# One eight-bank PSUM tile in place of four two-bank tiles, sinks split by two instructions a tile, and a new order, in a fused attention and soft-MoE kernel

## The chip, the cores and the metric

The kernel runs on one core of a Trainium2 chip. The metric is the time of one execution on the device in microseconds, the median of several runs. A core has five engines with instruction queues of their own: TensorE (PE, matmuls; its weight loads are listed as PEld), VectorE (DVE), ScalarE (ACT), GpSimd (POOL) and SyncE (SP, which issues most of the DMAs here). Each queue runs in order, and the engines wait for each other by semaphores. Matmul results lie in PSUM, which has eight banks of 512 floats a partition.

## The reference

Sliding-window attention with four sinks is followed by a soft mixture of experts; all is float32. There are 4 batches, 8 heads, 768 rows of 64; window 128; 8 experts with 4 slots each, model width 512, hidden width 1024.

```python
scores = scale * np.matmul(q, k.transpose(0, 1, 3, 2))
keep = (pos[None, :] < n_sink) | ((rel >= 0) & (rel < window))
a = softmax(np.where(keep, scores, -1e9))          # rows of 768
x = (a @ v).transpose(0, 2, 1, 3).reshape(B * S, H * D)
logits = x @ phi                                    # 3072 x 32
d = softmax(logits, axis=0)                         # over the 3072 tokens
slot_input = (d.T @ x).reshape(E, S_per_e, D)
h = np.maximum(slot_input[e] @ w1[e], 0.0)          # for each expert e
slot_out[e] = h @ w2[e]
return softmax(logits, axis=1) @ slot_out           # 3072 x 512
```

## The kernel before, in words

**Attention.** The work is cut into 12 jobs, one for each batch and each block of 256 rows, with all 8 heads. A job loads its k, q and v, transposes k and q on PE in 64x64 pieces (`prep`) and lets ACT and DVE copy them out of PSUM, and then goes through four score tiles (two groups of 64 rows a head by two sets of four heads): PE makes the scores, DVE masks them and takes the maxima, ACT the exponentials, DVE the inverse sums, POOL the normalised weights (`softmax`). POOL splits the weights of the four sinks into a high and a low half (`sinks`, L917: a cast and a subtraction for each of two pairs of heads), POOL cuts the window's triangle (`select`), PE transposes the weights and the sinks (the latter into `pst`), and `values` (L956) multiplies them with v. That product goes into two banks in two phases, `part(True)` and `part(False)`, with the PE drained between them; four matmuls for the sinks (pst by `vsink`) lie between. `natural` copies the result, and `moe.tokens` (L349) makes the logits of the job's tokens, their maxima, exponentials and weighted sums.

**Tail.** Behind the last job `finish` closes the sums over the tokens, and `tail` (L553) does the experts: 128 matmuls of the hidden product, relu by ACT (L573) and DVE (L574) on two tiles, transposes on PE with copies L593, further transposes with casts L547, then 168 matmuls of the second product, a split into high and low halves (L621 on ACT, L622 on DVE), and the output. The output is 24 tiles of 128x512, each one bank and two matmuls; the copies out of PSUM (L636) are ACT's for i = 0 and DVE's for i = 1, and seven DMAs of 0.5 or 1 MB (L637) take them to memory.

**What sets the order.** A planner (`Plan`, L168 to L296) is given each step with its engines, estimated times, what it reads and writes, and a key. Its loop picks, step by step, what can start first, with the keys as priorities; the numbers in the table `CFG` shift the keys. It hands each PSUM result one of eight banks, or two neighbouring ones for a score tile. The steps are issued in that order, by L129, and so the rows of the profile have this line for nearly everything. In the tail `InOrder` takes the place of the planner: a result gets the next of banks 2 to 7 in turn. The waits between engines are found afterwards, from which instruction touches which tile.

**Banks and tiles.** The eight banks are four tiles of two (L1225), and the bank with number b is a half of tile b // 2:

```python
pools = [ps.tile([P, 2, 512], F32, name=f"ps{i}") for i in range(4)]
...
t = self.banks[b // 2]
return t if kind == "s" else t[:, b % 2]
```

In the order of the kernel before, an instruction on one bank of such a tile waits for instructions on the other bank as well, even where the two results have nothing to do with each other.

Of the kernel before, what the change touches and what calls it, by code (L numbers as in the profile page):

```python
# [73 lines left out]
def sink_values(nc, plan, pool, tmp, c, v, v4s):  # L74

    B = v.shape[0]
    v4 = tmp[0:32, 0:256].rearrange("p (b d) -> p b d", b=B)
    srow = tmp[0:32, 512:640].rearrange("p (x r q z) -> p x r q z", x=2, r=4, q=2)
    hi = tmp[:, 768:1024].bitcast(F32R)
    c.v4s = v4s  # L80

    c.bm = pool.tile([P, 4], F32, name="bm")
    low = pool.tile([P, 1], F32, name="low")
    h = plan.psum()

    def load(e):
        for b in range(B):
            nc.sync.dma_start(v4[:, b, :], v[b, :, 0:NS, :])

    def selectors(e):  # L90
        sv = c.ident[0:32, 0:32].rearrange("p (q x z) -> p x q z", q=2, x=2)
        for r in range(4):
            nc.vector.tensor_copy(srow[:, :, r], sv)
        nc.vector.reduce_sum(c.bm, c.ident.rearrange("p (w q s) -> p q w s", w=8, q=4), axis=AX.XY)
        nc.vector.reduce_sum(low, c.ident.rearrange("p (x h z) -> p h x z", x=2, h=2)[:, 1], axis=AX.XY, negate=True)
# [12 lines left out]
    plan.add(1.0, "A", 0.3, lambda e: nc.scalar.copy(hi, h["tile"][:, 0:B * 64]), r=["v4p"], w=["v4h"])  # L108
    plan.add(1.0, "V", 0.8, split, r=["v4p", "v4h", "bm"], w=["v4s"], last=h)


def batch_sinks(nc, t, c, b):
    nc.vector.tensor_tensor(
        t.rearrange("p a (h d) -> p (a h) d", h=2),
        c.v4s[b].unsqueeze(1).to_broadcast([P, 4, 64]),
        c.bm.unsqueeze(2).to_broadcast([P, 4, 64]), op=ALU.mult)
# [26 lines left out]
class Plan:  # L143
# [24 lines left out]
    def add(self, key, eng, time, fn, r=(), w=(), new=None, last=None, mode=(128, 128), size=0):  # L168

        self.sizes.append(size)  # L170
        self.steps.append((key, eng, time if isinstance(time, tuple) else (time,) * len(eng), fn,
                           tuple(r), tuple(w), self.some(new), self.some(last)))
        self.modes.append(mode)

    def order(self):
# [41 lines left out]
        while len(order) < len(steps):  # L217
            best = None
            for e, o in todo.items():
# [17 lines left out]
                if at and (best is None or t0 < best[0]):  # L237
                    if e == "P":
                        _, t, i = min((steps[i][0] + self.STAY * (self.modes[i] != mode), t, i)
                                      for t, i in at if t <= t0 + 0.1)  # L240
# [5 lines left out]
            if e == "P":  # L246
                t0 += self.SWITCH * (self.modes[i] != mode)
                mode = self.modes[i]
            _, engs, times, _, _, _, new, last = steps[i]
# [72 lines left out]
class Moe:  # L322
# [26 lines left out]
    def tokens(self, plan, keys, b, j, x, xn, blocks):  # L349
# [34 lines left out]
        plan.add(next(k), "A", 0.34,  # L384
                 lambda e: nc.scalar.activation(lt[64:128], L["tile"][64:128, 0:P], AF.Exp, bias=new[64:128],
                                                accum_out=zb[64:128]),
                 r=[L["name"], ("m", n % 2)], w=["lt1", zbn], last=L)
        if n:

            plan.add(next(k), "A", 0.19,  # L390
                     lambda e: nc.scalar.activation(al, old, AF.Exp, bias=new, scale=-1.0),
# [42 lines left out]

        plan.add(next(k), "V", 0.14, totals, r=[zbn, aln], w=["z"])
        key = next(k)
# [51 lines left out]
    def slot_softmax(self, plan, key, b, names):  # L488
# [16 lines left out]

        plan.add(key, "V", 0.7, sums, w=[n])
        plan.add(key, "V", 0.3, lambda _: nc.vector.tensor_tensor(
            e, e, rs.unsqueeze(2).to_broadcast([P, 6, 32]), op=ALU.mult), w=[n])
# [131 lines left out]
class Weights:  # L640
# [9 lines left out]
    def load(self, t):  # L650
# [5 lines left out]
        else:  # L656
# [9 lines left out]
KIND = {'kt': 'w', 'q': 'w', 'T': 'w', 'sk': 'w', 'xn': 'w', 'x': 'w'}  # L666
CFG = {'prep': [58.14, -103.97, 8.81, 76.04, -10.47, 26.64],
       'load': [-48.35, 47.19],
       'v': [57.21, 53.78],
       'S': 15.41,  # L670
       'M': -22.38,
       'E': -97.66,
       'N': -54.45,
       'K0': -25.05,
       'T': [10.2, -41.41, 69.99, -71.23, -42.73, -20.91],
       'K': [-20.3, -9.37, 32.07],
       'sel': [-5.43, -51.93, -28.52, -10.71],
       'val': [36.09, 6.74, -33.7],
       'val1': [-174.01, 24.73, -66.86],
       'xn': [44.67, -22.43, -0.05],  # L680
       'tok': [89.38, -10.2, 18.38, -35.19, -40.54, -173.09, -194.1, 86.66, 85.8, -208.04,
               6.21],
       'sm': -1.2,
       'sinks': 12.15,
       'tr': [83.07, -55.05, -13.7, 82.62, 38.72, -58.7, 23.06, 2.13, -57.09, 43.08, 8.7, 2.71,
              59.56, 30.4, -103.15, -5.02, -84.19, 23.07, 51.64, 58.39, -12.0, -151.1, 31.83,
              47.24, -18.05, -22.13, 6.38],
       'w': [156.88, 8.0],
       'fin': [8.82, 115.48, -28.65, 1.18, 38.54, -142.25, -5.87, -1.81, -63.43, 24.51],
       'xn1': [-3.39, 43.09, -33.75],  # L690
       'tok1': [-8.95, -17.67, -75.74, 15.99, -33.99, 10.77, -17.8, 44.33, 18.88, -217.71,
                -10.41]}


def window_path(ctx, tc, c, moe, q, k, v, phi, w1, w2, out):
# [29 lines left out]
    v4s = [t[:, 1584 + 64 * b:1648 + 64 * b] for b in range(3)]  # L725
    skb = t[:, 1776:2032].rearrange("p (i x r q y s) -> p i x r q y s", i=2, x=2, r=4, q=2, y=2)
    t = slot()
# [5 lines left out]
    pts.append(fr.tile([P, 4, 132], F32, name="pt"))  # L733
    vsink = fr.tile([P, 2, P], F32R, name="vsink")
    pst = fr.tile([P, 256], F32R, name="pst")
# [115 lines left out]
    def softmax(keys, n, tl):  # L851
# [85 lines left out]
    def sinks_transposed(keys, n):  # L937
        h = turned(keys[0], KIND["sk"], lambda rows, m: skb[rows, m].rearrange("p x r q y s -> p (x r q y s)"),
                   [("sk", i, x) for i in range(2) for x in range(2)], n=2)
# [16 lines left out]
    def values(keys, n):  # L956
        b, j = jobs[n]
        opened, h = pair(KIND["x"])

        def part(first, last):  # L960

            for quad in range(2):
# [5 lines left out]
                for k in range(3):  # L968
                    for r, (m, o, w) in enumerate((lower[k], upper[k])):
# [5 lines left out]
                        for y in range(2):  # L975
                            nc.tensor.matmul(bank(h, x)[64 * y:64 * y + 64, at:at + w],
                                             lhsT=vbs[rows, m % 4, 4 * quad + 2 * x + y, :],
                                             rhs=xw[rows, 2 * x + y, o:o + w], start=first and k == 0 and quad == 0,
                                             stop=last, skip_group_check=True)
# [15 lines left out]
        add(keys[0], "P", 3.5 if j else 2.9, go, r=r, w=[x["name"] for x in opened], new=opened, mode=QUARTERS, size=200)  # L995
        for x in range(2):
# [224 lines left out]
def fused(ctx, tc, q, k, v, n_sink, window, phi, w1, w2, out):  # L1221
    nc = tc.nc
    B, H = q.shape[0:2]
    ps = ctx.enter_context(tc.tile_pool(name="ps", bufs=1, space=PSUM))
    pools = [ps.tile([P, 2, 512], F32, name=f"ps{i}") for i in range(4)]  # L1225
    keep = ctx.enter_context(tc.tile_pool(name="keep", bufs=1))
# [21 lines left out]

    t = pools[3][:, 1]
    for _ in range(WARM[0]):  # L1250
# [48 lines left out]
```

## Time and profile before

| | |
|---|---|
| median of 3 runs | 273.64 us (273.29 to 274.79) |
| the profiled execution | 276.34 us |
| its span, first to last instruction | 274.2 us |
| mean granted TensorE clock | 0.896 of full |
| attention, first job's start to last job's end | about 8 to 197 us |
| end of the last job's sums (`finish`) | 197 to 207 us |
| hidden product, relu and transposes | 207 to 226 us |
| second product | 226 to 243 us |
| output stage | 243 to 271 us |

The rows further below come from one profiled execution. A row of the chain of waits says which engine's work held up the end at that time; "issue" is time in which an engine waited for nothing that the profile shows. In a row of the timeline the bracket at the end says how long the engine had been idle, and whose work ended that. "ps" is PSUM; "wt" is the common name of the rotating buffers; "first" is another.

### The profile page before, as it was taken

What the parts mean: (1) busy time and instruction counts of PE and PEld (TensorE: products, weight loads), DVE (VectorE), ACT (ScalarE), POOL (GpSimd) and SP (SyncE); (2) the same over time, 40 slices, a digit from 0 to 9 for tenths busy, and PEclk for the clock granted to TensorE, in tenths of its full rate; (3) what the DMA queues carried; (4) which work ended last, traced back from release to release, by engine and by line L of the source; (5) the groups of instructions that cost most, each with busy time, mean ns of one, the idle gap of its engine ahead of it and who ended that gap; (6) DMA issues with size and microseconds to landing.
All of it is one profiled execution on the core that took longest, in us unless ns stands there. A gap on an engine that the chain in (4) does not pass through costs nothing.

```text
span 274.2 us, 9619 instructions
## 1 busy us (share of the span) xinstructions
PE 213.4 (78%) x3756; PEld 150.6 (55%) x3756; DVE 160.2 (58%) x439; ACT 148.3 (54%) x589; POOL 155.9 (57%) x377
## 2 busy tenths in 40 slices
PE   7648999878888877897987887865889959956550
PEld 7536676666665655675766665643663323435440
DVE  3478678598898586698769798653142131033330
ACT  2474858767878776587867787843141121022320
POOL 1148879959998957699885999869140500000000
PEclk9985699999999998899999999987699999985555
DMA  5497769998977684959796987934297999015564
GB/s 135 107 197 147 202 154 336 206 348 162 256 146 217 142 250 177 217 185 217 287 191 197 186 237 207 400 93 154 65 414 247 430 410 410 24 76 200 225 267 161
DMA packets 84504, 59.51 MB, mean 217 GB/s; under 512 B 76260, under 2 KB 76260, under 8 KB 82916
## 3 DMA queue, kind: packets, MB, share of 16 engines
q1 hardware_dynamic: 84452, 58.83, 72.8%
q8 instruction: 31, 0.51, 0.8%
q14 instruction: 21, 0.17, 0.2%
HBM read 52.53 MB, written 6.29 MB: 215 GB/s over the span
## 4 chain that ended last, share of the span: by engine, by line
PE 45%; DVE 22%; ACT 12%; POOL 9%; issue 9%; DVEq 0%; ACTq 0%; POOLq 0%
PE ps L129 43%; POOL wt L129 9%; DVE wt L129 7%; ACT wt L129 6%; DVE ps L129 5%; DVE wt L636 3%; DVE first L129 3%; ACT qt L129 2%; ACT first L129 2%; PE ps L1251 1%; DVE sums L129 1%; ACT lt L129 1%; DVE acc L129 1%; DVE call L129 0%; DVE qt L129 0%
## 5 line engine op out<-in xcount | busy, mean ns | idle before, releaser
L129 PE MATMUL ps<-wt 64*64 64x192 f32 (+6 forms) x1214 | 64.0, 325 | 14.5 <-DVE wt L636 6.6
L129 POOL TENSOR_TENSOR wt<-wt 128x16 f32<-128x16 f32 (+1 forms) x108 | 53.9, 505 | 24.0 <-DVE wt L129 15.9
L129 PEld LDWEIGHTS ps<-wt 64*64 64x64 f32 (+3 forms) x1214 | 45.9, 144 | 32.3 <-issue 11.6
L129 ACT ACTIVATE wt<-ps,wt 128x132 f32<-128x132 f32 x144 | 51.3, 374 | 13.1 <-DVE wt L129 12.2
L129 POOL TENSOR_SCALAR_AFFINE_SELECT wt<-wt 128x512 f32<-128x512 f32 x88 | 53.7, 636 | 3.2 <-DVE wt L129 1.4
L129 PE MATMUL ps<-wt,qt 64*64 64x196 f32 (+2 forms) x780 | 46.1, 341 | 8.4 <-ACT qt L129 3.2
L129 PEld LDWEIGHTS ps<-wt,qt 64*64 64x64 f32 x780 | 30.0, 142 | 19.0 <-POOL wt L129 4.8
L129 PE MATMUL ps<-ident,wt 64*128 64x64 f32 (+1 forms) x370 | 29.4, 248 | 8.3 <-DVE wt L129 3.5
L129 DVE TENSOR_REDUCE wt<-ps 128x4 f32<-128x528 f32 x48 | 34.0, 707 | 1.7
L129 ACT COPY wt<-ps 128x512 f32<-128x512 f32 x38 | 22.0, 593 | 23.1 <-PE ps L129 18.3
L129 PE MATMUL ps<-ident,first 64*128 64x64 f32 (+1 forms) x560 | 26.1, 232 | 8.0 <-DVE first L129 2.1
L129 PEld LDWEIGHTS ps<-ident,wt 64*128 64x128 f32 (+1 forms) x370 | 21.7, 150 | 19.1 <-POOL wt L129 7.4
L129 ACT ACTIVATION_READ_ACCUMULATOR wt<-ps,wt 128x1 f32 x144 | 30.1, 209 | 0.0
L129 PEld LDWEIGHTS ps<-ident,first 64*128 64x128 f32 (+1 forms) x560 | 21.8, 142 | 12.5 <-issue 2.5
L129 DVE COPY wt<-ps 128x512 f32<-128x512 f32 x34 | 22.7, 686 | 9.4 <-ACT first L129 3.0
L129 DVE COPY_PREDICATED ps<-later,ps 128x256 f32<-128x256 uint8 x48 | 20.3, 422 | 2.1 <-PE ps L129 1.1
L129 ACT COPY first<-ps 128x512 f32<-128x512 f32 x26 | 14.9, 590 | 11.6 <-PE ps L129 10.4
L129 DVE COPY first<-ps 128x512 f32<-128x512 f32 x22 | 14.8, 681 | 9.9 <-PE ps L129 8.3
L636 DVE COPY wt<-ps 128x512 f32<-128x512 f32 x12 | 8.3, 692 | 15.8 <-PE ps L129 15.8
L129 ACT ACTIVATE pt<-ps,wt 128x132 f32<-128x132 f32 x48 | 17.2, 384 | 0.5 <-DVE wt L129 0.2
L636 ACT COPY wt<-ps 128x512 f32<-128x512 f32 x12 | 7.0, 585 | 17.0 <-PE ps L129 17.0
L129 PE MATMUL ps<-first,phi 128*32 128x128 f32 x384 | 14.3, 295 | 2.1 <-ACT wt L129 1.9
(118 smaller groups left out, 278.7 us busy)
## 6 DMA issues: line engine op xcount, KB each, us to landing
wt<-in_moe_w_dram SPq DMA_DIRECT2D x30, 1024.0 KB, 8.6
wt<-in_v_dram SPq DMA_DIRECT2D x24, 256.0 KB, 5.2
first<-in_k_dram SPq DMA_DIRECT2D x22, 256.0 KB, 4.8
first<-in_q_dram SPq DMA_DIRECT2D x22, 256.0 KB, 5.3
out_dram<-wt SPq DMA_DIRECT2D x5, 1024.0 KB, 4.0
first<-in_moe_w_dram SPq DMA_DIRECT2D x2, 1024.0 KB
out_dram<-wt SPq DMA_DIRECT2D x2, 512.0 KB
first<-in_k_dram SPq DMA_DIRECT2D x4, 128.0 KB, 2.4
```

The lines of the kernel that those rows point to most:

```text
L129: return self.tc.keep_in_program_order(f(*args, **kw))
L636: (nc.vector.tensor_copy if i else nc.scalar.copy)(ob[:, n - n0, i], yp)
L1251: nc.tensor.matmul(t[:, 0:P], lhsT=c.ident, rhs=c.ident, start=True, stop=True)
```

## The change

Four things change. The eight banks become one tile, and a result is a slice of it. The sinks of a score tile are split by one cast and one subtraction of twice the width, with another layout of the buffers. Their product, still four matmuls, goes in two pairs, one ahead of each phase of `values`. The planner's cost of some steps is corrected and the table of keys replaced as a whole.

```diff
-    pools = [ps.tile([P, 2, 512], F32, name=f"ps{i}") for i in range(4)]
+    pools = ps.tile([P, 8, 512], F32, name="ps")
...
     def place(self, kind, b):
-        t = self.banks[b // 2]
-        return t if kind == "s" else t[:, b % 2]
+        return self.banks[:, b:b + 2] if kind == "s" else self.banks[:, b]
...
             o = 0 if odd else 128
-            for x in range(2):
-                sk = skb[:, odd, x, :, quad]
-                src = pt[:, 2 * x:2 * x + 2, o:o + 4].unsqueeze(1).to_broadcast([P, 2, 2, 4])
-                nc.gpsimd.tensor_copy(sk[:, 0:4:2].bitcast(F32R), src)
-                nc.gpsimd.tensor_tensor(sk[:, 1:4:2], src, sk[:, 0:4:2], op=ALU.subtract)
+            sk = skb[:, odd, quad]
+            src = pt[:, :, o:o + 4].unsqueeze(1).to_broadcast([P, 2, 4, 4])
+            nc.gpsimd.tensor_copy(sk[:, 0:4:2].bitcast(F32R), src)
+            nc.gpsimd.tensor_tensor(sk[:, 1:4:2], src, sk[:, 0:4:2], op=ALU.subtract)
...
+        def sunk(first):
+
+            for r in range(2):
+                x, rows = r if first else 1 - r, slice(64 * r, 64 * r + 64)
+                nc.tensor.matmul(bank(h, x)[:, 256 * r:256 * r + 256],
+                                 lhsT=vsink[rows, 2 * x:2 * x + 2, :].rearrange("p y d -> p (y d)"),
+                                 rhs=pst[rows], start=first, stop=False, skip_group_check=True)
+
         def go(e):
-            part(True, False)
-            for quad in range(2):
-                for x in range(2):
-                    rows = slice(64 * x, 64 * x + 64)
-                    nc.tensor.matmul(bank(h, x)[:, 256 * quad:256 * quad + 256], lhsT=vsink[rows, quad, :],
-                                     rhs=pst[rows], start=False, stop=False, skip_group_check=True)
-            nc.tensor.drain()
-            part(False, True)
+            for first in (True, False):
+                if not first:
+                    nc.tensor.drain()
+                sunk(first)
+                part(first)
...
-        plan.add(key, "V", 0.3, lambda _: nc.vector.tensor_tensor(
+        plan.add(key, "V", 0.9, lambda _: nc.vector.tensor_tensor(
...
-CFG = {'prep': [58.14, -103.97, 8.81, 76.04, -10.47, 26.64],
+CFG = {'prep': [19.45, -187.13, -2.19, 131.09, -1.42, 7.11],
...
```

**PE in the output stage.** Here is the queue of PE before where the output matmuls begin. The names ps_59, ps_60 and ps_61 are three of the two-bank tiles, and one row is one or two matmuls, two to a bank.

```order
L129 MATMUL ps_61<-wt 128x256 [waits DVE_49] x2
L129 MATMUL ps_59<-wt 128x256 x2
L129 MATMUL ps_59<-wt 128x256 [waits DVE_49]
L129 MATMUL ps_59<-wt 128x256
L129 MATMUL ps_60<-wt 128x256 x2
L129 MATMUL ps_60<-wt 128x256 [waits DVE_49]
L129 MATMUL ps_60<-wt 128x256
L129 MATMUL ps_61<-wt 128x256 [waits Activation_49]
```

And the same place after the change, where all banks have the name ps:

```order
L129 MATMUL ps<-wt 128x256 [waits DVE_49] x2
L129 MATMUL ps<-wt 128x256 x10
L129 MATMUL ps<-wt 128x256 [waits Activation_49]
L129 MATMUL ps<-wt 128x256
L129 MATMUL ps<-wt 128x256 [waits DVE_49]
L129 MATMUL ps<-wt 128x256
```

Before, the matmul into the second bank of a tile waits for an engine each time; after, twelve matmuls, six banks, stand ahead of the first wait for a copy.

**DVE in attention.** The queue of DVE before, in the middle of the first batch, where it copies out of three tiles and then sums up (the name first_78 is a buffer of that job):

```order
L129 COPY wt<-ps_61 128x4x128 [waits Activation_49]
L129 COPY wt<-ps_58 128x4x2x64 [waits Activation_49]
L129 COPY first_78<-ps_59 128x8x64 [waits Activation_49]
L129 TENSOR_REDUCE sums<-ps_61 128x1 [waits Activation_49]
L129 TENSOR_REDUCE sums<-sums 128x1 [waits DVE_49]
```

The same run of steps after:

```order
L129 COPY wt<-ps 128x4x128 [waits PE_49,Pool_49]
L129 COPY wt<-ps 128x4x2x64 [waits PE_49,Activation_49]
L129 COPY first_75<-ps 128x8x64 [waits PE_49]
L129 TENSOR_REDUCE sums<-ps 128x1 [waits PE_49]
L129 TENSOR_REDUCE sums<-sums 128x1 [waits DVE_49]
```

The copies and the first sum waited for ACT, and now wait for PE, one of them for ACT as well.

**PE at the values of a job.** PE's queue before, from the last scores to the second phase of a `values` in the first batch:

```order
L129 MATMUL ps_58<-wt,qt 64x196 [waits Activation_49]
L129 MATMUL ps_58<-wt,qt 64x196 x7
L129 MATMUL ps_61<-wt 64x192 [waits DMAHW0_49,DVE_49,Pool_49]
L129 MATMUL ps_61<-wt 64x192 x3
L129 MATMUL ps_61<-wt 64x64 [waits DMAHW7_49]
...
L129 MATMUL ps_61<-wt 64x128 x2
L129 MATMUL ps_61<-pst,vsink 128x256 x4
L129 MATMUL ps_61<-wt 64x192 x4
```

After, at the values of the fourth job:

```order
L129 MATMUL ps<-wt,qt 64x196 [waits Activation_49]
L129 MATMUL ps<-wt,qt 64x196 x7
L129 MATMUL ps<-pst,vsink 128x256 [waits DVE_49]
L129 MATMUL ps<-pst,vsink 128x256
L129 MATMUL ps<-wt 64x192 [waits DMAHW0_49,Pool_49]
L129 MATMUL ps<-wt 64x192 x3
...
L129 MATMUL ps<-wt 64x128 x2
L129 MATMUL ps<-pst,vsink 128x256 x2
```

Two of the four matmuls with pst have moved ahead of the window matmuls, with a wait of their own; the other two open the second phase.

## Rows read from the trace of the kernel before

**Rows 1.** The page's parts on the engines (of each the busy time, its share of the span and the number of instructions) and on the memory.

```profile
PE 213.4 (78%) x3756; PEld 150.6 (55%) x3756; DVE 160.2 (58%) x439; ACT 148.3 (54%) x589; POOL 155.9 (57%) x377
...
HBM read 52.53 MB, written 6.29 MB: 215 GB/s over the span
```

**Rows 2.** The page's chain of work that ended last, shares by engine.

```profile
PE 45%; DVE 22%; ACT 12%; POOL 9%; issue 9%; DVEq 0%; ACTq 0%; POOLq 0%
```

**Rows 3.** Stretches of the span: the length, then the busy time of PE, PEld, DVE, ACT and POOL with the number of instructions of each in brackets, the granted clock of PE, the DMA share and GB/s.

```profile
30.00:190.00 160.00, 132.33 (x2967) 100.32 (x2959) 121.53 (x324) 117.08 (x492) 133.12 (x315) 0.97 0.80 218
...
207.00:221.00 14.00, 13.92 (x129) 4.11 (x129) 1.83 (x5) 1.07 (x3) 3.83 (x7) 1.00 0.88 347
221.00:227.00 6.00, 3.13 (x25) 2.49 (x22) 2.26 (x7) 2.05 (x7) 0.00 (x0) 1.00 1.01 411
227.00:243.00 16.00, 14.52 (x164) 5.34 (x162) 1.76 (x6) 1.33 (x6) 0.00 (x0) 1.00 0.42 165
243.00:271.00 28.00, 14.06 (x47) 10.62 (x47) 8.31 (x13) 7.02 (x12) 0.00 (x0) 0.52 0.58 226
```

**Rows 4.** The chain of waits from the second product on, in order of time: start, us, what. It goes on in the same turns, 12 in all, to the last copy.

```profile
226.09 15.09 PE ps L129 x168
...
243.06 0.64 PE ps L129 x3
...
244.47 1.24 PE ps L129 x4
245.74 0.70 DVE wt L636
...
266.41 0.69 DVE wt L636
```

**Rows 5.** The waits by engine: who waited for whom, us in total, times, the longest.

```profile
PE ps L129 <- DVE wt L636: 9.2, 11, 0.9
...
PE ps L129 <- DVE wt L129: 8.0, 12, 2.6
```

**Rows 6.** Groups of instructions by line, engine, operation and shape: count, busy us and mean ns of one, idle time before them.

```profile
L129 POOL TENSOR_TENSOR wt<-wt 128x16 f32<-128x16 f32 x72 | 16.2, 225 | 5.8
L129 POOL CAST wt<-wt 128x16 fp32r<-128x16 f32 x72 | 14.4, 199 | 1.0
...
L129 POOL TENSOR_TENSOR wt<-call,wt 128x128 fp32r<-128x128 f32 x6 | 2.8, 458 | 0.5
...
L129 POOL CAST wt<-call 128x128 fp32r<-128x128 f32 x6 | 1.7, 289 | 6.4 <-PE ps L129 6.4
...
L129 PE MATMUL ps<-pst,vsink 64*128 64x256 f32 x48 | 6.3, 343 | 0.0
...
L636 DVE COPY wt<-ps 128x512 f32<-128x512 f32 x12 | 8.3, 692 | 15.8 <-PE ps L129 15.8
```

**Rows 7.** Stretches of one microsecond in the output stage, with the columns of rows 3.

```profile
252.00:253.00 1.00, 0.32 (x1) 0.32 (x2) 0.63 (x1) 0.04 (x1) 0.00 (x0) 0.50 1.05 422
...
254.00:255.00 1.00, 0.25 (x1) 0.25 (x2) 0.69 (x1) 0.10 (x1) 0.00 (x0) 0.50 0.10 37
...
256.00:257.00 1.00, 0.19 (x1) 0.19 (x2) 0.69 (x1) 0.17 (x1) 0.00 (x0) 0.50 0.99 401
...
271.00:272.00 1.00, 0.00 (x0) 0.00 (x0) 0.00 (x0) 0.00 (x0) 0.00 (x0) 0.50 0.09 25
```

**Rows 8.** The timeline's row for the first output DMAs: start, us, engine and line.

```profile
244.48 6.53 SPq L637 DMA_DIRECT2D out_dram<-wt  x3
```

**Rows 9.** The timeline between the two products of the experts.

```profile
221.09 0.69 ACT L573 ACTIVATE wt<-ps,rz 128x512 f32<-128x512 f32 x1 [6.15 <-PE ps L129]
...
221.81 0.75 DVE L574 TENSOR_SCALAR wt<-ps,rz 128x512 f32<-128x512 f32 x1 [6.09 <-ACT wt L573]
...
223.25 0.93 PE L129 MATMUL ps<-ident,wt 128*128 128x128 f32 x6 [1.59 <-DVE wt L593]
```

**Rows 10.** The chain of waits from the last job's values to the hidden product.

```profile
197.37 0.70 DVE first L129
...
198.14 0.38 ACT wt L129
...
204.12 0.49 DVE acc L129
204.63 0.38 ACT qt L129
...
207.08 13.98 PE ps L129 x128
```

**Rows 11.** The chain of waits between 30 and 50 us: its shares, and three of its pieces.

```profile
by line: PE ps L129 62.3%; DVE first L129 10.5%; issue 7.9%; DVE wt L129 7.2%; ACT first L129 6.1%; DVE ps L129 3.9%; ACT wt L129 3.0%; DVE call L129 1.1%
...
34.77 0.60 ACT first L129
...
35.39 0.70 DVE first L129
...
36.13 0.73 PE ps L129 x16
```

**Rows 12.** The timeline at two places of one job in the second batch.

```profile
94.88 1.09 ACT L129 ACTIVATE qt<-ps 128x512 f32<-128x512 f32 x2 [1.66 <-PE ps L129]
...
101.22 1.55 PE L129 MATMUL ps<-wt 64*64 64x192 f32 x48 [1.53 <-ACT wt L129]
```

More of the change, by code (lines that the diff above doesn't have):

```diff
@@ L113, in batch_sinks @@
     nc.vector.tensor_tensor(
-        t.rearrange("p a (h d) -> p (a h) d", h=2),
+        t,
         c.v4s[b].unsqueeze(1).to_broadcast([P, 4, 64]),
@@ L172, in add @@
                            tuple(r), tuple(w), self.some(new), self.some(last)))
-        self.modes.append(mode)
+        self.modes.append(mode if isinstance(mode[0], tuple) else (mode, mode))
     def order(self):
@@ L238, in order @@
                     if e == "P":
-                        _, t, i = min((steps[i][0] + self.STAY * (self.modes[i] != mode), t, i)
+                        _, t, i = min((steps[i][0] + self.STAY * (self.modes[i][0] != mode), t, i)
                                       for t, i in at if t <= t0 + 0.1)
@@ L246, in order @@
             if e == "P":
-                t0 += self.SWITCH * (self.modes[i] != mode)
-                mode = self.modes[i]
+                t0 += self.SWITCH * (self.modes[i][0] != mode)
+                mode = self.modes[i][1]
             _, engs, times, _, _, _, new, last = steps[i]
@@ L383, in tokens @@
         plan.add(next(k), "A", 0.16, lambda e: nc.scalar.copy(lt[0:64], L["tile"][0:64, 0:P]), r=[L["name"]], w=["lt0"])
-        plan.add(next(k), "A", 0.34,
+        plan.add(next(k), "A", 0.46,
                  lambda e: nc.scalar.activation(lt[64:128], L["tile"][64:128, 0:P], AF.Exp, bias=new[64:128],
@@ L388, in tokens @@
         if n:
-            plan.add(next(k), "A", 0.19,
+            plan.add(next(k), "A", 0.28,
                      lambda e: nc.scalar.activation(al, old, AF.Exp, bias=new, scale=-1.0),
@@ L433, in totals @@
                 nc.vector.tensor_tensor(z[64:96], z[64:96], zb[64:96], op=ALU.add)
-        plan.add(next(k), "V", 0.14, totals, r=[zbn, aln], w=["z"])
+        plan.add(next(k), "V", 0.3, totals, r=[zbn, aln], w=["z"])
         key = next(k)
@@ L504, in sums @@
             nc.vector.reciprocal(rs, rs)
-        plan.add(key, "V", 0.7, sums, w=[n])
-        plan.add(key, "V", 0.3, lambda _: nc.vector.tensor_tensor(
+        plan.add(key, "V", 1.05, sums, w=[n])
+        plan.add(key, "V", 0.6, lambda _: nc.vector.tensor_tensor(
             e, e, rs.unsqueeze(2).to_broadcast([P, 6, 32]), op=ALU.mult), w=[n])
@@ L666 @@
 KIND = {'kt': 'w', 'q': 'w', 'T': 'w', 'sk': 'w', 'xn': 'w', 'x': 'w'}
-CFG = {'prep': [58.14, -103.97, 8.81, 76.04, -10.47, 26.64],
[L668 to L692, printed above, removed]
@@ new lines @@
+CFG = {'prep': [19.45, -187.13, -2.19, 131.09, -1.42, 7.11],
+       'load': [-8.46, -1.5],
+       'v': [9.11, -1.32],
+       'S': -4.43,
+       'M': -11.99,
+       'E': -56.88,
+       'N': -145.77,
+       'K0': -39.56,
+       'T': [-78.79, 20.93, -15.94, -27.31, -38.74, -41.02],
+       'K': [-4.0, -54.79, 17.1],
+       'sel': [-61.44, 12.04, 9.99, -1.14],
+       'val': [14.63, -23.95, 0.59],
+       'val1': [-24.06, -170.69, 162.59],
+       'xn': [144.17, 122.98, 22.1],
+       'tok': [252.15, -9.05, -112.26, -63.98, -31.24, -31.82, -5.09, 58.15, 114.14, -99.52,
+               -19.39],
+       'sm': 2.99,
+       'sinks': -3.08,
+       'tr': [80.19, -20.41, 41.42, 110.05, 13.47, 6.41, -97.51, -1.24, -13.15, -0.56, -6.74,
+              -14.57, 106.06, -3.25, -143.31, -49.34, -4.56, -19.02, 154.9, -271.99, 1.16,
+              128.12, -28.68, -35.86, -78.07, 3.97, -90.14],
+       'w': [19.2, 8.0],
+       'fin': [32.37, -133.68, -96.25, 132.41, -24.83, 127.81, 43.86, 12.76, -163.2, 56.42],
+       'xn1': [55.18, -279.24, -17.3],
+       'tok1': [-59.2, 8.13, 25.59, -36.2, -27.54, -46.4, -10.28, -31.83, 19.85, -100.11,
+                35.89]}
@@ L733, in window_path @@
     pts.append(fr.tile([P, 4, 132], F32, name="pt"))
-    vsink = fr.tile([P, 2, P], F32R, name="vsink")
+    vsink = fr.tile([P, 4, D], F32R, name="vsink")
     pst = fr.tile([P, 256], F32R, name="pst")
@@ L937, in sinks_transposed @@
     def sinks_transposed(keys, n):
-        h = turned(keys[0], KIND["sk"], lambda rows, m: skb[rows, m].rearrange("p x r q y s -> p (x r q y s)"),
+        h = turned(keys[0], KIND["sk"], lambda rows, m: skb[rows, m].rearrange("p q r a s -> p (q r a s)"),
                    [("sk", i, x) for i in range(2) for x in range(2)], n=2)
@@ L958, in values, with part @@
         opened, h = pair(KIND["x"])
-        def part(first, last):
+        def part(first):
             for quad in range(2):
@@ L977, in part @@
                                              lhsT=vbs[rows, m % 4, 4 * quad + 2 * x + y, :],
-                                             rhs=xw[rows, 2 * x + y, o:o + w], start=first and k == 0 and quad == 0,
-                                             stop=last, skip_group_check=True)
-        def go(e):
-            part(True, False)
-            for quad in range(2):
-                for x in range(2):
-                    rows = slice(64 * x, 64 * x + 64)
-                    nc.tensor.matmul(bank(h, x)[:, 256 * quad:256 * quad + 256], lhsT=vsink[rows, quad, :],
-                                     rhs=pst[rows], start=False, stop=False, skip_group_check=True)
-            nc.tensor.drain()
-            part(False, True)
+                                             rhs=xw[rows, 2 * x + y, o:o + w], start=False, stop=not first,
+                                             skip_group_check=True)
+        def sunk(first):
[4 more added lines that the diff above has]
+                                 rhs=pst[rows], start=first, stop=False, skip_group_check=True)
+        def go(e):
+            for first in (True, False):
[3 more added lines that the diff above has]
+                part(first)
         r = [("xw", quad, i, w) for quad in range(2) for i in range(2) for w in range(2)]
@@ L994, in values @@
             r += [("vb", (2 * n - 1) % 4)]
-        add(keys[0], "P", 3.5 if j else 2.9, go, r=r, w=[x["name"] for x in opened], new=opened, mode=QUARTERS, size=200)
+        add(keys[0], "P", 3.5 if j else 2.9, go, r=r, w=[x["name"] for x in opened], new=opened, mode=(HALVES, QUARTERS), size=200)
         for x in range(2):
@@ L1246, in fused @@
     moe.first = first
-    t = pools[3][:, 1]
+    t = pools[:, 7]
     for _ in range(WARM[0]):
```

10 lines of the change are left out of this document (5 added, 5 removed).

## The prediction

> **What bounds the kernel now.** I read the busy shares first: PE 78% of 274.2 us, every other engine under 59% [rows 1]. That mean hides stages. The chain that ended last is 45% PE, 22% DVE, 12% ACT and 9% POOL [rows 2], so nearly half of the time some other engine holds the end up. The table by stage shows where: attention from 30 to 190 us has PE busy 132.3 and POOL 133.1 of 160 us, the first product of the experts (207 to 221) and the second (227 to 243) are PE at over 90%, but in the output stage, 243 to 271, PE is busy 14.1 of 28 us, DVE 8.3, ACT 7.0, and DMA 58% [rows 3]. Nothing there is full.
>
> The chain says why: four matmuls (1.24 us), DVE copy (0.70), four matmuls, DVE copy, in strict turns, a round each 2.07 us (245.74 to 266.41 in ten, [rows 4]). A round makes two output tiles of one bank each, one copied by ACT, one by DVE. The order of the kernel before explains the turns: the third matmul of a round writes the other bank of a tile whose first bank DVE is still copying, and waits for that copy, though no data is shared. The waits view puts 9.2 us of PE on those copies, 11 times [rows 5].
>
> **The output stage.** In the new order PE's first output matmuls wait once, then ten go without a wait, and each later wait is for the copy made six banks earlier. ACT and DVE lose their waits for each other too. So PE runs ahead and the copies (DVE 692 ns, the slower one, [rows 6]) can follow each 0.75 us: 12 rounds in 9 us at full clock. What is late next is the transfer: 6.29 MB leave the chip. A microsecond in which transfers overlap moves 401 to 422 GB/s, one between moves 37 [rows 7]. At 400 that is 15.7 us from about 245.2 (first issue at 244.48, [rows 8]), so to 260.9, against 271.1 now, where the share falls to 0.09: -10.2 us. The cover for this is production ahead of the queue. The granted clock in this stage is 0.50, the lower of the two levels (1.2 GHz), behind 1.9 us in which PE waited (241.2 to 243.06) and then worked in turns; at that clock a round is 1.24 us on PE, 0.64 + 11 x 1.24 from 243.06 ends at 257.3, the last copy at 258.1, and the last 1 MB, 3.9 us on its way today (issued behind the last copy's end at 267.1), lands at 262.0: -9.1. Ends -11 and -8; I take -10.2, since both bounds come close to it.
>
> The Trainium skill weighs in here twice. "DMA: Bandwidth & Descriptors" (Specifications) gives HBM about 358 GB/s a core; by that the transfer takes an estimated 17.6 us, and the stage gains 8.3 instead of 10.2. The rows of this trace pass that figure in every microsecond at full share, so the measurement decides. "TensorE: Matmul & The Clock Gate" (A second HAM failure mode: psum-queue depth-cycling) says that an engine that idles briefly between groups while it goes through the PSUM banks keeps losing its clock; the 0.50 beside the turns agrees, and with fewer pauses it would rather rise than fall. If it stays low the sum is the -9.1 above.
>
> **Relu, transposes, turns (221.1 to 226.1).** DVE's relu begins at 221.81 when ACT's ends, 0.70 late, as its half lies in the sibling bank of ACT's; PE's next transposes then stand 1.59 us for a DVE copy of the sibling bank [rows 9]. In the new program neither wait is there. Sum -2.3; ends -0.7 (the copies are late next) and -3.5. The second product could start that much earlier: its weights load at 411 GB/s through this stage, and the share of 0.42 in the 16 us behind it puts the last of them some 7 us into the product, where PE, 91% busy, waits for none [rows 3]; I count no loss.
>
> **The last job's end (197.4 to 207.1).** 9.7 us of short steps, most of them on ACT and DVE in turn [rows 10]. Some follow a read of the sibling bank, as ACT's copy at 198.14 behind DVE's of 197.37, and ACT's at 204.63 behind DVE's at 204.12; each such turn costs 0.4 to 0.7. Three of them: -1.5; ends 0 and -3.5, since the order here is new as well.
>
> **Attention, waits.** From 34.77 ACT copies one bank, from 35.39 DVE the other, from 36.13 PE makes the next transposes: 0.6 to 0.7 us which the new program puts side by side. At 94.88 ACT copies qt 1.66 us after its idle time began, for PE's logits in the sibling bank; at 101.22 PE's values begin after 1.53 us idle, when ACT's exponentials of the neighbour are read [rows 11, 12]. The pieces named, 1.66, 1.53 and two of 0.65 for the copies, are 4.5 us; I take that as an estimate for one of four batches, 18 in all. The new DVE order shows the same copies and sums waiting for PE, and only one of them for ACT as well.
>
> **Attention, POOL.** 72 casts of 199 ns and 72 subtractions of 225 take 30.6 us, and 24 more of each, on another buffer, make it 40.8; they become 48 and 48 of double size. For a cast of 128x32 the rows give 199 at 16 columns and 289 at 128, so 199 to 289, taken 212; for a subtraction 225 at 16, 458 at 128, taken 258 [rows 6]. 48 x 0.47 = 22.6 us, so POOL is rid of 18 us of 156, 1.5 a job; it holds 9% of the chain. At the bounds (289, 458) it would still save 5 us, at (199, 225) 20.5.
>
> **Attention, the sinks' product.** The matmuls are as many as before: 48 of 128x256 at 343 ns [rows 6]. Half of them now open the product instead of following its first phase, so pst and vsink, written by ACT and DVE, must be there some 1.5 us earlier (the first phase's 48 matmuls took 1.55 us at 101.22, [rows 12]); PE's queue behind it holds the 48 to 96 window matmuls and whatever the planner put next. Before, the plan let the whole step wait for pst too, and PE's idle time before these matmuls is 0.0. Zero; ends -1 and +18 (12 x 1.5). The DMAs of q, k, v and weights are the same in number; v of the first job is issued earlier; DMA share in attention is 0.80, which a stage 10 us shorter raises to 0.85.
>
> **Attention, sum.** The waits and POOL's saving overlap, and what goes from one engine shows up on the next: PE is busy 132 of 160 us already, which makes 27.7 the most that could go [rows 3], and POOL, DVE and the loads each hold part of that. A new order can also lose. Ends +2 and -20; I take a third of PE's idle time, -9.
>
> **Sum.** -10.2 - 2.3 - 1.5 - 9 = -23.0. The profiled execution took 276.34 us (span 274.2, 2.1 around it), 2.7 over the median of the runs, 273.64. I take the difference off the median: 250.6 us (253.3 profiled).
>
> **Rivals.** One: attention stays as long as it is, because the loads (mean share 0.80) and POOL set its pace and the new order only shifts the gaps; for it, POOL's 83%, against it, waits that share no data are on the chain itself. Then -14: 259.6. Two: the order follows the freed banks, and attention comes near PE's floor, -20: 239.6; for it, 62.3% of the chain at 30 to 50 us is PE already [rows 11], against it the loads. Three, slower: the in-order queue of PE gets a new head wait in each job, at the sinks' product that now opens the values: pst comes from POOL's split by a transpose and a copy, and everything that PE could do meanwhile stands behind it. PE's longest wait for DVE's copies in the view is 2.6 us [rows 5]; 12 x 2.6 = 31 us against the 23 of the forecast gives 281.8. It decides from 1.9 us a job on. Against it, the split is half as long now. Four: the copies in the output stage don't run ahead, since something other than the bank holds them (an output buffer that waits for an old weight, say), and the new order of attention brings nothing: 273 to 274. Against it, the waits named in the order of PE.
>
> **How the numbers follow.** Forecast, attention -4 to -15: 0.59, own range 244 to 256. Rival one 0.18, two 0.15, three 0.04, four 0.02; 0.02 for a mix of one and three that ends at 262 to 272. A range from 241 to 262 leaves out half of two, all of three and four, half of the mix: about 0.15. Under 0.5% (1.4 us) a measurement of this kernel can't tell from no change. Faster 0.94, same 0.02, slower 0.04.
>
> **What would show it.** In the new profile: the waits of PE for L636's copies (now L635) gone from the list; six tiles made before the first pause; DMA share near 1.0 from 246 us on the old scale for 15 us without gaps, and the span's last 3 us as before; DVE's relu beside ACT's; second product 2 us after the relu rather than 4.3; POOL's casts and subtractions of 128x32 48 each, near 212 and 258 ns; attention, from 30 us to the last job's end, 9 us shorter with PE's share at 87%. The prediction is wrong if the output stage still takes over 20 us, or if PE's longest waits in attention are for pst or vsink.

## The result, and the profile of the changed kernel

The changed kernel takes 242.29 us (median; 240.57 to 244.24) against 273.76, ratio 0.8825 with a 95% interval of 0.8754 to 0.8896: 31.5 us faster. The forecast was 250.6 us. Medians are over all executions, ratios leave out those in a slower state that some executions show, so the two don't divide out exactly. The result is inside the stated range (241 to 262), and outside the likeliest case's own range (244 to 256).

The page of the changed kernel shows the busy times, and the shares of the chain that ended last:

```profile
span 238.9 us, 9509 instructions
...
PE 203.1 (85%) x3754; PEld 143.5 (60%) x3754; DVE 157.3 (66%) x444; ACT 147.7 (62%) x584; POOL 140.4 (59%) x281
...
PE 52%; DVE 18%; DMA 8%; ACT 7%; issue 7%; POOL 2%; SPq 0%; DVEq 0%; ACTq 0%; POOLq 0%
```

Beside [rows 1, 2] POOL lost 15.5 us of work and its share of the chain fell from 9% to 2%; PE went from 45% to 52% of a shorter span, and a DMA is on the chain for the first time, the load of a weight that the second product waits for.

Four marks of the timeline cut the span into stages; they were read in the same way for every kernel below. "Last values" is the end of the last window matmul of attention, "hidden" the first matmul of the hidden product, "second" the end of the second product, "output" the first output matmul that needs the whole split.

| us | last values | hidden starts | second ends | output starts | span ends |
|---|---|---|---|---|---|
| before | 196.95 | 207.08 | 241.14 | 243.06 | 274.2 |
| changed | 176.06 | 183.43 | 215.51 | 217.42 | 238.9 |

So attention is 20.9 us shorter, the end of the last job 2.8 (10.1 to 7.4), hidden product to second product 2.0 (34.1 to 32.1), output 9.7 (31.1 to 21.5). That is 35.3 of span, while the medians differ by 31.5: the profiled execution of before lay 2.6 over its median and the changed one's 1.7 under its own, so some 4 us of these differences are scatter; if all of it lies in attention, attention is 17 us shorter by the medians. The forecast counted the output stage to the end of the full transfer (243.06 to 271.1, 28 us) and not to the span's end; so measured it takes 18.2 us now (217.42 to some 235.6), 9.9 less and under the 20 that would have spoken against it. The table by stage and the microseconds of the output stage, columns as in [rows 3]:

```profile
30.00:169.00 139.00, 129.32 (x2951) 96.88 (x2947) 119.02 (x327) 117.34 (x487) 116.14 (x221) 1.00 0.88 242
...
218.00:219.00 1.00, 1.00 (x10) 1.00 (x9) 0.92 (x2) 1.00 (x3) 0.00 (x0) 0.84 0.00 0
219.00:220.00 1.00, 1.00 (x6) 1.00 (x6) 0.97 (x2) 0.82 (x2) 0.00 (x0) 0.50 0.32 127
220.00:221.00 1.00, 1.00 (x7) 1.00 (x6) 0.79 (x2) 0.73 (x2) 0.00 (x0) 0.50 1.01 406
...
222.00:223.00 1.00, 1.00 (x10) 1.00 (x10) 0.99 (x2) 0.82 (x2) 0.00 (x0) 0.95 1.03 418
...
235.00:236.00 1.00, 0.00 (x0) 0.00 (x0) 0.00 (x0) 0.00 (x0) 0.00 (x0) 0.50 0.57 213
```

PE is busy 93% of attention, where it was 83% and the forecast had 87%. In the output stage data flows at full share (0.94 to 1.08 in each microsecond) from 220 to 235 without a gap, against [rows 7], where the share was 0.10 between two transfers. Part of the gain is TensorE's clock: PE made the same matmuls (3756 and 3754) in 203.1 us instead of 213.4, and the mean granted clock of the profiled execution is 0.951 instead of 0.896. Some 7 us of these 10 lie in the output stage, where [rows 3] had a clock of 0.52, and 3 in attention; what the clock alone is worth to attention was not tried. The timeline of the tail answers to [rows 4, 9]:

```profile
174.51 1.55 PE L129 MATMUL ps<-wt 64*64 64x192 f32 x48
...
183.43 12.64 PE L129 MATMUL ps<-wt,si 128*32 128x512 f32 x114
...
196.58 0.69 ACT L572 ACTIVATE wt<-ps,rz 128x512 f32<-128x512 f32 x1 [6.18 <-PE ps L129]
...
197.30 2.70 PE L129 MATMUL ps<-ident,wt 128*128 128x128 f32 x22
197.44 0.75 DVE L573 TENSOR_SCALAR wt<-ps,rz 128x512 f32<-128x512 f32 x1 [6.09 <-PE ps L129]
...
212.73 2.78 PE L129 MATMUL ps<-wt 128*32 128x256 f32 x44 [1.00 <-DMA wt<-in_moe_w_dram]
...
217.42 4.30 PE L129 MATMUL ps<-wt 128*128 128x256 f32 x23 [0.54 <-DVE wt L621]
217.84 1.60 ACT L635 COPY wt<-ps 128x512 f32<-128x512 f32 x3 [0.99 <-PE ps L129]
218.08 2.66 DVE L635 COPY wt<-ps 128x512 f32<-128x512 f32 x4 [0.72 <-PE ps L129]
```

DVE's relu waits for PE alone, no longer for ACT: it begins right behind the hidden product's end (197.37), where it used to begin 0.8 us behind it (221.81 against 221.02). It doesn't run beside ACT's, as the forecast had it, since ACT's own now begins before that product ends. PE makes 22 transposes in one go; the output matmuls run 23 in a row with copies of both engines beside them. One new wait has come: PE stands 1.00 us in the second product for a weight. Its load is on the chain, issued during the hidden product as before:

```profile
194.43 18.26 DMA wt<-in_moe_w_dram
```

### The profile page after: what moved, and what is told of

Its sections match the earlier page's. It is cut to its first block, busy times and chain, and to the rows that moved or that the text cites. A ratio compares the mean times of both kernels' runs of the same rounds, so it can differ in the third digit from the quotient of the medians.

```text
span 238.9 us, 9509 instructions
## 1 busy us (share of the span) xinstructions
PE 203.1 (85%) x3754; PEld 143.5 (60%) x3754; DVE 157.3 (66%) x444; ACT 147.7 (62%) x584; POOL 140.4 (59%) x281
## 4 chain that ended last, share of the span: by engine, by line
PE 52%; DVE 18%; DMA 8%; ACT 7%; issue 7%; POOL 2%; SPq 0%; DVEq 0%; ACTq 0%; POOLq 0%
PE ps L129 51%; DMA wt<-in_moe_w_dram 8%; DVE wt L129 6%; DVE ps L129 5%; ACT wt L129 4%; POOL wt L129 2%; PE ps L1254 2%; DVE rs L129 1%; DVE wt L635 1%; DVE first L129 1%; DVE sums L129 1%; DVE acc L129 1%; ACT pt L129 1%; ACT qt L129 1%; DVE qt L129 0%
## 5 line engine op out<-in xcount | busy, mean ns | idle before, releaser
L129 PE MATMUL ps<-wt 64*64 64x192 f32 (+6 forms) x1214 | 58.2, 314 | 2.8 <-DVE wt L621 1.5
L129 POOL TENSOR_TENSOR wt<-wt 128x528 f32<-128x528 f32 (+1 forms) x72 | 47.1, 663 | 21.1 <-DVE wt L129 15.1
L129 PEld LDWEIGHTS ps<-wt 64*64 64x64 f32 (+3 forms) x1214 | 40.8, 137 | 17.0 <-issue 6.9
L129 ACT COPY wt<-ps 128x512 f32<-128x512 f32 x42 | 24.2, 594 | 16.2 <-PE ps L129 12.7
L129 PE MATMUL ps<-ident,wt 64*128 64x64 f32 (+1 forms) x370 | 25.7, 241 | 3.5 <-DVE wt L129 3.1
L129 PEld LDWEIGHTS ps<-ident,wt 64*128 64x128 f32 (+1 forms) x370 | 20.3, 146 | 11.4 <-POOL wt L129 6.8
L129 DVE COPY first<-ps 128x512 f32<-128x512 f32 x23 | 15.6, 686 | 12.3 <-PE ps L129 11.9
L129 DVE COPY wt<-ps 128x512 f32<-128x512 f32 x30 | 20.2, 683 | 1.9 <-PE ps L129 1.1
L129 POOL TENSOR_TENSOR pt<-pt,wt 128x528 f32<-128x528 f32 x12 | 13.1, 1090 | 1.6 <-ACT wt L129 0.8
L129 PE MATMUL ps<-wt,si 128*32 128x512 f32 x120 | 13.9, 593 | 0.0
L129 PE MATMUL ps<-first,phi 128*32 128x128 f32 x384 | 13.4, 276 | 0.3
```

Of the source, the lines that this page charges most:

```text
L129: return self.tc.keep_in_program_order(f(*args, **kw))
```

## The experiments

The change has three parts that can be had apart: the tile, the split and product of the sinks, and the order. All kernels below are timed against the kernel before on the same chip; every ratio has its 95% interval. Two theories stand against each other. Mine: the waits between sibling banks are the larger part, and shorten attention too. The rival: they explain the tail, and attention is shorter because of the new order.

**The tile alone.**

```diff
-    pools = [ps.tile([P, 2, 512], F32, name=f"ps{i}") for i in range(4)]
+    pools = ps.tile([P, 8, 512], F32, name="ps")
...
-        t = self.banks[b // 2]
-        return t if kind == "s" else t[:, b % 2]
+        return self.banks[:, b:b + 2] if kind == "s" else self.banks[:, b]
```

> The kernel before with the one eight-bank tile and nothing else; order, sinks and product as before. If the waits between sibling banks are the larger part: output stage -9.7 us, relu and transposes -2.4, attention and its end -10 or more, about 250 us. If the new order is what shortens attention: the same in the tail, attention within 3 us of before, about 260.

Measured: 249.44 us, ratio 0.9071 (0.8977 to 0.9164), so 24 us faster. Marks: 183.33, 191.41, 223.84, 225.75, 247.2. The output stage takes 21.45 us, as in the changed kernel, and attention is 13.6 us shorter than in the profile of before, 10 by the medians (23.7 less the 13.4 that the stages behind the last values gained). My theory has it, at its own number. The timeline of its last values, its hidden product and its output stage:

```profile
181.78 1.55 PE L129 MATMUL ps<-wt 64*64 64x192 f32 x48
...
191.41 12.22 PE L129 MATMUL ps<-wt,si 128*32 128x512 f32 x112 [0.46 <-ACT wt L129]
...
225.75 3.10 PE L129 MATMUL ps<-wt 128*128 128x256 f32 x23 [0.54 <-DVE wt L621]
226.17 6.53 ACT L635 COPY wt<-ps 128x512 f32<-128x512 f32 x12 [0.99 <-PE ps L129]
226.41 7.27 DVE L635 COPY wt<-ps 128x512 f32<-128x512 f32 x12 [0.71 <-PE ps L129]
```

Each engine does its twelve copies in one go, ACT in 6.5 us and DVE in 7.3, where [rows 4] had a round each 2.07 us. But the chain of this kernel, by engine, has a new entry:

```profile
PE 31%; DVE 18%; POOL 17%; ACT 12%; issue 9%; DMA 8%; SPq 0%; POOLq 0%; ACTq 0%; DVEq 0%
```

POOL, with the same instructions as before, went from 9% to 17% of the chain. My reading is that with the false waits gone, PE, DVE and ACT come to it sooner, and it holds them up; the runs with the split below test it.

**All but the tile.**

```diff
-    pools = ps.tile([P, 8, 512], F32, name="ps")
+    pools = [ps.tile([P, 2, 512], F32, name=f"ps{i}") for i in range(4)]
...
-        return self.banks[:, b:b + 2] if kind == "s" else self.banks[:, b]
+        t = self.banks[b // 2]
+        return t if kind == "s" else t[:, b % 2]
```

> The changed kernel with four tiles of two banks again: new order, split and product without the freed banks. If the waits between sibling banks are the larger part: the tail goes back to 31 us of output and 5 us of relu and transposes, and attention is as long as before or longer, 265 to 275 us. If the order and the split carry attention by themselves: only the tail comes back, 12 us over the changed kernel, about 254.

Measured: 270.26 us, ratio 0.989 (0.9826 to 0.9955). The output stage is back at 30.6 us and its turns are back on the chain:

```profile
242.49 1.24 PE ps L129 x4
243.78 0.04 issue
243.82 0.70 DVE wt L636
244.52 0.04 issue
244.57 1.24 PE ps L129 x4
```

Split, product and order together are worth 3 us under the false waits (273.16 to 270.26), and 7 without them (249.44 to 242.29).

**The old table and old costs in the changed kernel.** This was meant to give the old order with the new split.

```diff
-CFG = {'prep': [19.45, -187.13, -2.19, 131.09, -1.42, 7.11],
+CFG = {'prep': [58.14, -103.97, 8.81, 76.04, -10.47, 26.64],
...
-        plan.add(key, "V", 0.9, lambda _: nc.vector.tensor_tensor(
+        plan.add(key, "V", 0.3, lambda _: nc.vector.tensor_tensor(
```

> The changed kernel with the old table of keys and the old costs: one tile, the split by two and the product in two pairs. If the order was worth little: within 3 us of the changed kernel, 242 to 245. If the new order is worth the 11 us of attention by which the forecast fell short: about 253.

Measured: 248.47 us, ratio 0.9086 (0.9036 to 0.9135). It lies between the two numbers, and it turned out to test neither: the changed planner is told that the values open in one PE mode and end in another (HALVES and QUARTERS, the planner's names for how a matmul divides TensorE's array), and with that the old table gives an order that is neither the old one nor the new.

**The new table and costs with one tile and the old sinks.** The same holds the other way round. The tile and the costs of the changed kernel are in this run too.

```diff
...
-CFG = {'prep': [58.14, -103.97, 8.81, 76.04, -10.47, 26.64],
+CFG = {'prep': [19.45, -187.13, -2.19, 131.09, -1.42, 7.11],
...
```

> The kernel before with one tile and the new table and costs, but the old split (four instructions a tile) and the old product. If POOL's 18 us were on the path: 250 to 255. If they only filled idle time of POOL: 242 to 246. The order was not made for this split, which speaks for the higher end.

Measured: 270.72 us, ratio 0.9901 (0.9869 to 0.9934), above both ends. The last values end at 205.61, 22 us later than with the tile alone. The stages show where, columns as in [rows 3]:

```profile
90.00:110.00 20.00, 15.08 (x257) 11.41 (x252) 11.52 (x31) 9.81 (x42) 12.55 (x35) 0.78 0.79 263
110.00:130.00 20.00, 16.54 (x322) 12.02 (x322) 12.26 (x32) 10.59 (x49) 11.18 (x22) 0.91 1.05 297
...
170.00:190.00 20.00, 17.46 (x395) 13.26 (x399) 17.12 (x52) 17.61 (x80) 17.04 (x39) 1.00 0.23 70
```

All engines are busy for less of the time from 90 to 130 us than later, while the DMAs move 263 to 297 GB/s; later, from 170 to 190, they move 70. Which load was late was not tried. The planner, its keys and its costs belong together: the same table, with one thing told otherwise, is worth 24 us less, as the run with exactly the new order below shows.

**Exactly the old order, with the new split and product.** To the run with the old table and costs, one more edit: the planner is told of one mode again, and so issues the steps in the order of the kernel before. In the traces ACT's 589 instructions come in that kernel's order one for one, and DVE's but for one.

```diff
-        add(..., new=opened, mode=(HALVES, QUARTERS), size=200)
+        add(..., new=opened, mode=QUARTERS, size=200)
```

> One tile, the split by two and the product in two pairs, in exactly the order of the kernel before (the earlier run with the old table had another order, since the planner was told of the product's modes). If POOL's 18 us lie beside other work: within 1.5 us of the one-tile kernel, 248 to 250. If they are on the path: 242 to 245.

Measured: 244.08 us, ratio 0.8944 (0.8842 to 0.9047), and in five more rounds, with the changed kernel beside it:

> One tile, new split and new product in the order of the kernel before, once more. If the new order is worth something by itself: 1.5 to 3 us over the changed kernel. If not: within 1 us of it.

> The changed kernel once more, unedited, beside the next two on one chip in five rounds: 240 to 244 us.

This time 242.68 us, ratio 0.8803 (0.8738 to 0.8867), and for the changed kernel 241.60 us, ratio 0.8811 (0.8767 to 0.8856). With the new split, the new order is worth nothing that can be measured. Split and product take 5 to 7 us from the tile alone. The chain by engine of the kernel with the old order (first run) is close to that of the changed kernel:

```profile
PE 42%; DVE 22%; ACT 12%; DMA 8%; issue 7%; POOL 3%; SPq 0%; DVEq 0%; ACTq 0%; POOLq 0%
```

POOL 3% (5% in the second profile), where the tile alone had 17%.

**Exactly the new order, with the old split and product.** To the run with the new table, costs and old sinks, one more edit: the planner gets the pair of modes as well; the code of sinks and product stays the old one. In the traces ACT's and DVE's instructions come in the changed kernel's order one for one.

```diff
-        add(..., new=opened, mode=QUARTERS, size=200)
+        add(..., new=opened, mode=(HALVES, QUARTERS), size=200)
```

> One tile and exactly the order of the changed kernel, with the old split of four instructions and the old product. If the order alone is worth the 7 us between the one-tile kernel and the changed one: 242 to 245. If the order pays only with the shorter split: 248 or more.

Measured: 246.51 us, ratio 0.9033 (0.8953 to 0.9113), between the two numbers expected and not told apart from the tile alone (0.9071) by the intervals. The waits of PE's weight loads and the chain by engine:

```profile
PEld ps L129 <- POOL wt L129: 19.4, 28, 3.0
```

```profile
PE 33%; POOL 31%; DVE 10%; issue 9%; DMA 8%; ACT 4%; POOLq 0%; SPq 0%; DVEq 0%; ACTq 0%
```

POOL is 31% of the chain, nearly as much as PE; in the changed kernel, in the same order, the same wait is 9.3 us and POOL's share 2%. The wait by itself doesn't say this: in the kernel before it was 19.4 us too, with POOL at 9% of the chain.

**The split alone, four instructions again.**

```diff
-            sk = skb[:, odd, quad]
-            src = pt[:, :, o:o + 4].unsqueeze(1).to_broadcast([P, 2, 4, 4])
+            for x in range(2):
+                sk = skb[:, odd, quad, :, 2 * x:2 * x + 2]
+                src = pt[:, 2 * x:2 * x + 2, o:o + 4].unsqueeze(1).to_broadcast([P, 2, 2, 4])
```

> The changed kernel with four instructions a tile for the split of the sinks, its order and product untouched: 18 us more of POOL. On POOL's path: 248 or more. Beside other work: 242 to 244.

Measured: 248.27 us, ratio 0.9072 (0.8982 to 0.9162), 6 to 7 us slower than the changed kernel's runs, and the intervals of the ratios don't touch; chain by engine:

```profile
PE 41%; POOL 20%; DVE 12%; DMA 8%; issue 7%; ACT 6%; SPq 0%; POOLq 0%; DVEq 0%; ACTq 0%
```

The edit has an order and a product that are the changed kernel's to the instruction, so the 6 us are the split's. That the ratio is the tile alone's (0.9071) and not told apart from that of the new order with the old split and product (0.9033), which differs from it in the product, leaves no price for the product that can be measured. The split's groups in this kernel, and then in the changed one:

```profile
L129 POOL TENSOR_TENSOR wt<-wt 128x16 f32<-128x16 f32 x72 | 16.7, 232 | 5.8
L129 POOL CAST wt<-wt 128x16 fp32r<-128x16 f32 x72 | 14.5, 202 | 0.7
```

```profile
L129 POOL TENSOR_TENSOR wt<-wt 128x32 f32<-128x32 f32 x36 | 9.3, 260 | 2.9
L129 POOL CAST wt<-wt 128x32 fp32r<-128x32 f32 x36 | 7.6, 211 | 0.7
...
L129 POOL TENSOR_TENSOR wt<-pt,wt 128x32 f32<-128x32 f32 x12 | 3.0, 251 | 1.0
L129 POOL CAST wt<-pt 128x32 fp32r<-128x32 f32 x12 | 2.5, 208 | 0.0
```

The changed kernel's four groups sum to 22.4 us, against 40.8 before.

**The first pair of the sinks' matmuls behind the first phase.**

```diff
-            for first in (True, False):
-                if not first:
-                    nc.tensor.drain()
-                sunk(first)
-                part(first)
+            part(True)
+            sunk(True)
+            nc.tensor.drain()
+            sunk(False)
+            part(False)
```

> The changed kernel with the first pair of the sinks' matmuls behind the first phase's window matmuls instead of ahead of them. If PE waits for pst at the opening of the values (rival three, in small): 1 to 3 us less, 239 to 241. If the wait is covered, as the forecast had it: 241 to 243.

Measured: 240.68 us, ratio 0.883 (0.8752 to 0.8907). A gain of 1.6 us by the medians, none by the ratios; so it was run again, beside the changed kernel.

> The changed kernel with the first pair of the sinks' matmuls behind the first phase, once more. If the pair at the opening costs: 1 to 2 us less than the changed kernel. If that was scatter: within 0.7 us of it.

Now 241.60 us, as the changed kernel to the hundredth, ratio 0.8833 (0.8786 to 0.8881). It was scatter. PE's idle time ahead of the values, pair and window matmuls together, is 3.7 us in the profile of the changed kernel, where the pair opens them, and 4.1 in the second one of this kernel, where it follows. None of these kernels beats the changed one by more than the scatter.

**Two banks for the output tiles.**

```diff
+                    pool.at = 2 + i
                     yp = pool.tile()
```

> The changed kernel with two banks in turn for the output tiles instead of six, ACT's tiles always in one and DVE's in the other; each matmul waits for the copy of its own bank alone. If the sibling waits were what made the turns: a round of one matmul pair and one copy, 1.1 to 1.4 us, so production ends after 13 to 17 us, and the output stage is 0 to 3 us longer than with six. If the run ahead over six banks is what counts: rounds near 2 us again, 8 us or more longer.

Measured: 244.26 us, ratio 0.8927 (0.8878 to 0.8976), 2 to 3 us over the changed kernel. Output stage from 218.02 to the span's end at 242.8: 24.8 us, 3.3 more than with six banks and just over the 0 to 3 expected. Its chain has rounds of one tile and one copy:

```profile
228.32 0.81 PE ps L129 x2
229.13 0.02 issue
229.15 0.70 DVE wt L636
229.85 0.04 issue
229.90 0.81 PE ps L129 x2
```

1.58 us a round here, over the 1.1 to 1.4 expected, but not 2.07: PE fills one engine's bank while the other engine copies. So two banks without false waits beat six with them: 6.3 of the 9.7 us come back with the waits alone, and the last 3.3 need more than two banks.

## Why the prediction was right in direction and short in size

**Output stage, -10.2: right.** -9.7 in the profile, with the tile alone too. The mechanism was the one named, and the next limit was the one named: the transfer. It ran at 385 to 418 GB/s in the microseconds at a share of 1.00 or more. The Trainium skill states 358 for a core ("DMA: Bandwidth & Descriptors", Specifications); by that figure the stage would have been an estimated 2 us longer. The bound from PE at half clock did not decide: the clock was low for only 3.4 us of PE's work, and in the tile alone, where it was not low, the stage is as long.

**Relu, transposes, turns, -2.3 with no loss behind: -2.0, by two misses that cancel.** From the hidden product's end to the second product's start it was 6.2 us and is 2.6: -3.6, just beyond the end of -3.5. The second product itself took 14.0 us and takes 15.6, 1.0 of it standing for a weight. "I count no loss" was wrong by 1.6: the last loads are issued during the hidden product, as before, so they did not come earlier with the relu's gain. That the sum is nearly met is luck.

**The last job's end, -1.5: -2.8**, inside the ends. With the tile alone in the old order it was 8.1 us long against 10.1, so 2.0 of it are the tile's.

**Attention, waits: the mechanism right, the size between its two numbers.** The tile alone took about 10 us from attention by the medians, against a first estimate of 18 for these waits and the -9 of the whole sum. Which of the waits named gave how much was not tried.

**Attention, POOL: the duration right, the place wrong.** The forecast's 212 and 258 ns were 211 and 260, its 22.6 us in all 22.4. But the step that failed is that of the sum of attention, "The waits and POOL's saving overlap, and what goes from one engine shows up on the next", at -9. Attention lost 17 us by the medians, not 9. What goes from one engine did show up on the next: freed of the false waits, the kernel had POOL on 17% of its chain. But the saving there did not overlap with the waits: it was worth about 6 us, and it came on top of their 10 instead of being part of them. Under the false waits split, product and order together gave 3. The forecast took POOL's 9% of the old chain as its weight, where the chain to look at was the one that would be left. Sum as measured by the medians: 24 for the tile, 6 to 7 for the split, together 30 to 31 of the 31.5.

**The sinks' product, 0: right in time.** It can't be told from 0 in either position. But "The matmuls are as many as before" did not mean as much work: PE's busy time for these 48 went from 6.3 us [rows 6] to 9.9, and its idle time before them from 0.0 to 3.4, while that before the window matmuls went from 6.4 to 0.3. Rival three, a new head wait of 2 us and more a job, did not occur: the longest wait of PE in attention from 30 us on is 1.1 us.

**The order.** The forecast left it inside attention's -9 without a price. Its price can't be told from 0, with the new split or with the old. Rival two came nearest in time (239.6 against 242.3), and its reason was wrong: not the order brought attention close to PE's floor but tile and split, in the old order as well. Rival one, attention as long as before because of loads and POOL, is refuted for the loads (DMA share rose from 0.80 to 0.88 and attention still shrank) and half right about POOL.

The range held because it reached to rival two; the case that I called likeliest ended at 244. That the number fell inside is in part luck: the sum was some 8 us short.

## What to carry to other kernels

Where two results share a tile, look in the program's order for waits between them and on the chain for turns of two engines; one tile of all banks, cut into slices, gave 24 us of 274 here. When a wait is taken off several engines, weigh the savings on the others by the chain that will be left, not by the chain as it is: an engine at 83% busy and 9% of the chain was the next bound. And a searched table of priorities is worth what it is worth only with the costs and rules it was sought with; compare two tables with the issued order held fixed.

## What the runs showed of the hardware

TensorE's clock fell to the lower level (0.50 of full, 1.2 GHz) just before 219 us in the output stage of the changed kernel although PE was busy in every microsecond from 218 on; before that, from 215.5 to 217.4, it had waited for the split with 0.4 us of work. Soon after 222 it was back at 2.4 GHz, while PE stayed busy. With the tile alone the same waits (0.99 and 0.54 us) lie ahead of the same matmuls, and the clock stayed at 1.00: 23 matmuls took 3.10 us there and 4.30 here. So these waits don't decide it by themselves, and what does is open. The Trainium skill ("TensorE: Matmul & The Clock Gate", A second HAM failure mode: psum-queue depth-cycling) lays a clock that swings to brief pauses between groups of matmuls. In the kernel before it did not swing: it stayed at 0.50 through the turns. Here the fall came inside a stretch without pauses, and nothing but PE's own time paid for it: the stage is 21.5 us long in both kernels, since the transfer set the end.

As the forecast had it, a split in two POOL instructions instead of four costs little more than half: 128x32 takes 211 ns where 128x16 takes 199 (casts), and 260 where it takes 225 (subtractions). Between these two widths most of POOL's time is in the number of instructions.
